# Lower steps for the last weights' pieces, the first tile's softmax first, half of the last stores on the scalar engine

## The chip, the cores and the metric

One NeuronCore of one Trainium2 chip runs the whole program. The metric is the device time of one execution in microseconds (us). Engines in the profile: PE is the tensor engine's matmuls, PEld its weight loads, DVE the vector engine, ACT the scalar engine, POOL the GpSimd engine, SP the sync engine, which issues all the DMAs of the kernel before (SPq in the rows).

## The reference

Two attention blocks with 32 learned queries, then two MLPs on 12480 tokens of 128 features with 2048 hidden features:

```
h  = softmax(I x^T / sqrt(128)) x          # I: 32 x 128, x: 12480 x 128
a  = softmax(x h^T / sqrt(128)) h          # 12480 x 128
y1 = (relu(a w_in) + alpha * min(a w_in, 0)) w_out
y2 = relu(y1 w2_in)^2 w2_out
```

The four weights come as float64 and are converted on the chip from their two 32-bit halves; x, the queries and alpha are float32.

## The kernel before

**Tiling.** The second attention and the two MLPs run over 30 tiles of 416 tokens; the hidden features are cut in 16 chunks of 128. The main loop has a step for each pair of a tile and a chunk (480, plus some at the end). At step s, `l1_a(s)` computes a chunk of the first MLP's hidden features (L575), `l2_a` a chunk of the second MLP's (L593 to L595, 24 steps later), and `l1_b` and `l2_b` add earlier chunks into the outputs y1 and y2 (L604 for the first tile, else L593 to L595). Products at full precision take three matmuls of float32r halves (hi and lo): ACT writes hi, DVE or POOL writes lo.

**Banks.** `l1_a` of the first 24 steps writes one of four PSUM banks in turn, so step s waits until ACT and DVE have read the bank of step s - 4. `l2_a(0)` at step 24 needs y1 of the first tile as `y1h` (ACT, L616) and `y1l` (DVE, L618), which follow `end_y1(0)` at step 22.

**Order.** Tile's scheduler is off (`manual_schedule`): each engine works through its instructions in program order. What does not belong to the loop's body is dealt to steps by `at(step, f)`, and runs at the end of that step's list.

**The weights' pieces.** Each weight is converted in pieces of 512 columns. `load_w` issues a DMA of 512 KB into one of four `raw` buffers (SP; L154 for w_out and w2_out, L158 for w_in and w2_in), and waits there until POOL is through with that buffer's last piece. `to_f32` has four stages: magnitude (ACT, L172, needs the DMA), low (ACT, L175), bits (DVE, L179), sign (DVE L183, then POOL L184). A fifth stage splits the result in hi and lo (ACT L218 or L204, or DVE L218; then POOL L189). For w_out there is one more POOL instruction between (L199, `aw`). `convs[4]` to `convs[7]` are the four pieces of w_out. The eight pieces of w2_in and w2_out are dealt by the table `PIECES`: piece n does its stages at five steps, and when four stages are done the load of piece n + 3 is issued. Pieces 0, 1, 2 and 4 are of w2_in, pieces 3, 5, 6 and 7 of w2_out.

**The second attention's tiles.** `first` is the softmax of tile 0: scores (PE, L435), a chain on DVE with one exponential on ACT (L443 to L465), a spreading matmul (L489), a split into `a_s` (L496, L498). Without `a_s` step 0 cannot start. `second` is the softmax of tiles 1 to 3 in six steps and a split: `a_hi` on ACT (L474), `a_lo` on POOL (L189), and twelve DMAs from SP (L480) that copy both into three `a_s` tiles. Tile 1 is needed at step 16.

**The product of the weights.** `step_u` (PE, L550, steps 11 to 14), `copy_u` (ACT, L557, `u_sb`, step 15) and `step_v` (PE, L561, step 16) form a small matrix that `end_y1` uses. L561 stands in PE's queue between the matmuls of step 16, and waits for `u_sb`.

**The end.** The last tile's y2 is transposed by DVE (L653) and stored by four DMAs from SP (L657).

Of the kernel before, what the change touches and what calls it, by code (L numbers as in the profile page):

```python
# [28 lines left out]
def attention_then_two_mlps(ctx: ExitStack, tc, x, inducing, w_in, w_out, alpha, w2_in, w2_out, out):  # L29
# [3 lines left out]
    nc = tc.nc  # L33
# [6 lines left out]
    NT = N // T  # L40
# [150 lines left out]
    def conv_w_in(k):  # L191
        return to_f32("w_in", k, lambda: w_in_sb[:, k * 512 : (k + 1) * 512])

    def conv_w_out(k):
        chunks, cols = slice(4 * k, 4 * k + 4), slice(k * 512, (k + 1) * 512)
        f, hi, lo, a = (v.rearrange("p c d -> p (c d)")[:, cols] for v in (w_out_sb, wo_hi, wo_lo, aw))

        def rest():
            nc.gpsimd.tensor_tensor(  # L199
                aw[:, chunks], w_out_sb[:, chunks], al1[:, chunks].unsqueeze(2).to_broadcast([P, 4, P]), op=ALU.mult  # L200
            )

        def split():
            nc.scalar.copy(hi, a)  # L204
            pool_lo(lo, a, hi)

        return to_f32("w_out", k, lambda: f) + [rest, split]
# [56 lines left out]
    last = len(groups1) - 1  # L264
# [65 lines left out]
    def run(fs):  # L330
        for v in fs:
            v()

    convs = [conv_w_in(k) for k in range(4)] + [conv_w_out(k) for k in range(4)]
# [32 lines left out]
    def transpose_w_in(k):  # L367
        b = y2_bank()
        for i in range(4):
            c = 4 * k + i  # L370
            nc.tensor.transpose(b[:, i * P : (i + 1) * P], w_in_sb[:, c * P : (c + 1) * P], ident)
        for i in range(4):
            c = 4 * k + i
            nc.scalar.activation(
                wiT[:, c * P : (c + 1) * P], b[:, i * P : (i + 1) * P], AF.Copy, scale=al[:, c : c + 1]
            )
# [37 lines left out]
        den.unsqueeze(1).to_broadcast([P, Q, M]), op=ALU.mult,  # L414
    )
    transpose_w_in(1)
    run(convs[5][2:4])
    convs[4][4]()


    a_s = {}
# [84 lines left out]
    def make_w1s(k):  # L506
        w1_bank[k] = x_banks[k]() if k < 2 else y2_bank()
        nc.tensor.matmul(w1_bank[k], hT, w_in_sb[:, k * 512 : (k + 1) * 512], start=True, stop=True)

    def split_w1s(k, low):  # L510
        dst, b = w1s[:, k * 512 : (k + 1) * 512], w1_bank[k]
        if low:
            nc.vector.tensor_tensor(dst[64:], b[64:], f32(dst[64:]), op=ALU.subtract)
        else:
            nc.scalar.copy(dst, b)

    first = second_attention([0], [0, P, 2 * P, T - P])
    second = second_attention([1, 2, 3])
    first[0]()
    make_w1s(0)  # L520
    transpose_w_in(2)
    run(convs[6][:2])
    run(first[1:4])
    split_w1s(0, 0)
    second[0]()
    transpose_w_in(3)
    stage1.close()
    make_w1s(1)
    convs[5][4]()
    run(first[4:6])  # L530
    split_w1s(0, 1)
    first[6]()
    convs[6][2]()
    first[7]()
    convs[6][3]()
    convs[6][4]()
    second[1]()
    split_w1s(1, 0)
    load_w("w2_in", 0)
    load_w("w2_in", 1)  # L540
# [51 lines left out]
    def three(b, w_hi, w_lo, hi, lo, start, stop):  # L592
        nc.tensor.matmul(b, w_hi, hi, start=start, stop=False)  # L593
        nc.tensor.matmul(b, w_lo, hi, start=False, stop=False)  # L594
        nc.tensor.matmul(b, w_hi, lo, start=False, stop=stop)  # L595
# [46 lines left out]
    def l2_b(i):  # L642
        t, c = divmod(i, NCH)
        if c == 0:
            y2_cur[t] = y2_bank()
        b = y2_cur[t][:, :T]
        hi, lo = g2.pop(i)
        cols = slice(c * P, (c + 1) * P)
        three(b, w2[2][:, cols], w2[3][:, cols], hi, lo, c == 0, c == NCH - 1)
        if c == NCH - 1:  # L650

            o = wk.tile([P, T], F32, name="o", tag="o", bufs=2)
            nc.vector.transpose(o, b)  # L653
            del y2_cur[t]
            dst = out[t * T : (t + 1) * T, :].rearrange("(b i) (a j) -> a i b j", i=M, j=M)
            for a in range(P // M):
                nc.sync.dma_start(  # L657
                    out=dst[a], in_=o[a * M : (a + 1) * M, :].rearrange("i (b j) -> i b j", j=M)
                )

# [1 line left out]
    SPLIT1, U_AT = [9, 11, 15, 18], [11, 12, 13, 14]  # L662

    PIECES = [
        (6, 15, "w2_in", 0), (9, 17, "w2_in", 1), (12, 19, "w2_in", 2), (15, 22, "w2_out", 0),
        (18, 24, "w2_in", 3), (21, 27, "w2_out", 1), (24, 30, "w2_out", 2), (28, 34, "w2_out", 3),
    ]
    total = NT * NCH
    plan = {}
# [1 line left out]
    def at(s, f, *a):  # L671
        plan.setdefault(s, []).append(lambda: f(*a))

    at(1, split_w1s, 1, 1)
    at(0, second[2])
    at(2, make_w1s, 2)
    at(2, split_w1s, 2, 0)
    at(2, second[3])
    at(2, second[4])
    at(5, split_w1s, 2, 1)  # L680
    at(4, second[5])
    at(2, convs[7][0])
    at(5, convs[7][1])
    at(5, convs[7][2])
    at(5, make_w1s, 3)
    at(5, split_w1s, 3, 0)
    at(7, split_w1s, 3, 1)
    at(7, second[6])
    at(7, convs[7][3])
    at(8, convs[7][4])  # L690
    for k in range(4):
# [23 lines left out]
    def stages(parts, steps):  # L715
        for v, s in zip(parts, steps):
            at(s, v)

    at(3, load_w, *PIECES[2][2:])


    def piece(n):
        s, last, name, k = PIECES[n]
        stages((conv_w2_in if name == "w2_in" else conv_w2_out)(k), [s, s + 1, s + 2, s + 3, last])
        if n + 3 < len(PIECES):
            at(s + 4, load_w, *PIECES[n + 3][2:])

    for n in range(len(PIECES)):
        at(PIECES[n][0] - 1, piece, n)
    l1_b_at = {}  # L730
    for i in range(total):
        early = max(0, min(LAG1_EARLY - LAG1, (LAG2 - 1 - i) // 2))
# [1 line left out]
    for s in range(total + LAG2 + LAG2B + 4):  # L734
        if s < total:
            l1_a(s, s < LAG2 and s % 2)
        if 0 <= s - LAG2 < total:
            l2_a(s - LAG2)
        if 0 <= s - LAG2 - 1 < total:
            l2_split(s - LAG2 - 1)  # L740

        ends = [(l1_b, i) for i in l1_b_at.get(s, [])]
        if 0 <= s - LAG2 - LAG2B < total:
            ends.insert(0 if ends and ends[0][1] % NCH == 0 else len(ends), (l2_b, s - LAG2 - LAG2B))
        for f, i in ends:
            f(i)
        for f in plan.pop(s, []):
            f()
# [30 lines left out]
```

## Time and profile before

| | |
|---|---|
| runs | 990.95, 991.48, 992.05 us; median 991.48 |
| the profiled execution | 992.0 us, of which the span from first to last instruction is 990.2 |
| busy share of the span | PE 98%, PEld 95%, ACT 77%, DVE 69%, POOL 56% |
| chain that ended last | PE 95%, DVE 1%, ACT 1%, DMA 1%, POOL 1% |
| granted TensorE clock, mean | 0.993 |

The 1.8 us between the span and the profiled execution's time lie around the program. A row of the trace has the start in us, the duration in us, the engine, the line, the operation, output and inputs, the count, and in brackets the idle time of the engine before it with what ended it. PE's matmuls overlap: two that follow each other at full speed start 0.19 us apart.

### The profile page before, as it was taken

The numbers are of one execution on the slowest core, as the hardware profiler recorded it, in microseconds if no ns is written. First come the engines' busy times: TensorE is split into PE (matmuls) and PEld (weight loads), VectorE is DVE, ScalarE is ACT, GpSimd is POOL, SyncE is SP. The second block draws the span as 40 slices with busy tenths as digits, with TensorE's granted clock in tenths as the row PEclk, the third lists the DMA queues.
The fourth block names the chain that finished last, engine by engine and source line by source line (L and its number), as shares of the span: only waits on it lengthen the run. The fifth ranks groups of instructions, "written<-read, shape, count | busy, mean of one in ns | idle before, by whom it ended". The sixth has DMA issues, their size and how long they took to land.

```text
span 990.2 us, 16031 instructions
## 1 busy us (share of the span) xinstructions
PE 971.3 (98%) x5325; PEld 937.3 (95%) x5325; DVE 685.1 (69%) x1199; ACT 762.0 (77%) x1584; POOL 556.4 (56%) x518
## 2 busy tenths in 40 slices
PE   7898999999999999999999999999999999999997
PEld 5667999999999999999999999999999999999997
DVE  4778876667666677666776667766677666776677
ACT  4757787777877777777777777777777777777776
POOL 1367766555655556555565555655556555565530
PEclk9988999999999999999999999999999999999999
DMA  9431002000010000100001000010000100010001
GB/s 315 159 97 58 1 9 44 10 10 2 10 42 10 10 9 5 40 10 10 10 12 33 10 10 10 18 27 10 9 9 23 23 10 10 9 27 1 10 9 19
DMA packets 66356, 28.42 MB, mean 29 GB/s; under 512 B 54224, under 2 KB 62176, under 8 KB 66272
## 3 DMA queue, kind: packets, MB, share of 16 engines
q1 hardware_dynamic: 66272, 27.39, 11.2%
q8 instruction: 42, 0.69, 0.3%
q14 instruction: 42, 0.34, 0.1%
HBM read 14.80 MB, written 6.39 MB: 21 GB/s over the span
## 4 chain that ended last, share of the span: by engine, by line
PE 95%; DVE 1%; ACT 1%; DMA 1%; POOL 1%; issue 0%; SPq 0%; ACTq 0%; POOLq 0%; DVEq 0%
PE y L595 18%; PE y L594 18%; PE y L593 18%; PE h L595 9%; PE h L593 9%; PE h L594 9%; PE h L575 9%; PE h L243 1%; PE ms L255 1%; PE ms L435 1%; DMA xg<-in_x_dram 1%; PE y L614 1%; PE y L316 1%; DMA raw<-in_moe_w_out_dram 0%; PE y L307 0%
## 5 line engine op out<-in xcount | busy, mean ns | idle before, releaser
L639 POOL TENSOR_TENSOR g2l<-sq,g2h 128x416 fp32r<-128x416 f32 x456 | 495.6, 1088 | 346.3 <-ACT g2h L637 235.7
L589 DVE SCALAR_TENSOR_TENSOR g1l<-h,g1h 128x416 fp32r<-128x416 f32 x464 | 274.0, 590 | 223.0 <-ACT g1h L587 218.5
L587 ACT ACTIVATE g1h<-h 128x416 fp32r<-128x416 f32 x464 | 240.4, 519 | 138.7 <-PE h L575 131.5
L631 DVE TENSOR_TENSOR sq<-h,r 128x416 f32<-128x416 f32 x480 | 283.6, 591 | 48.1 <-ACT r L629 3.0
L629 ACT ACTIVATE r<-h 128x416 f32<-128x416 f32 x480 | 249.1, 519 | 53.3 <-PE h L595 6.6
L637 ACT CAST g2h<-sq 128x416 fp32r<-128x416 f32 x480 | 255.0, 531 | 1.9 <-DVE sq L631 1.9
L575 PE MATMUL h<-a_s,w1s 128*128 128x416 f32 (+1 forms) x480 | 173.5, 363 | 2.3 <-DVE a_s L498 1.2
L595 PE MATMUL h<-y1l,w2i_hi 128*128 128x416 f32 x480 | 168.4, 351 | 1.3 <-DVE y1l L618 1.3
L593 PE MATMUL h<-y1h,w2i_hi 128*128 128x416 f32 x480 | 168.3, 351 | 1.0 <-DVE g1l L589 1.0
L595 PE MATMUL y<-g2l,w2o_hi 128*128 128x416 f32 x480 | 168.7, 351 | 0.0
L594 PE MATMUL h<-y1h,w2i_lo 128*128 128x416 f32 x480 | 168.6, 351 | 0.0
L594 PE MATMUL y<-g2h,w2o_lo 128*128 128x416 f32 x480 | 168.0, 350 | 0.0
L593 PE MATMUL y<-g2h,w2o_hi 128*128 128x416 f32 x480 | 167.7, 349 | 0.0
L595 PE MATMUL y<-g1l,wo_hi 128*128 128x416 f32 x464 | 163.1, 351 | 0.0
L594 PE MATMUL y<-g1h,wo_lo 128*128 128x416 f32 x464 | 162.7, 351 | 0.0
L593 PE MATMUL y<-g1h,wo_hi 128*128 128x416 f32 x464 | 162.4, 350 | 0.0
L575 PEld LDWEIGHTS h<-a_s,w1s 128*128 128x128 f32 (+1 forms) x480 | 90.8, 190 | 13.5 <-DVE sq L631 4.8
L593 PEld LDWEIGHTS h<-y1h,w2i_hi 128*128 128x128 f32 x480 | 90.2, 188 | 3.2 <-ACT y1h L616 1.2
L595 PEld LDWEIGHTS h<-y1l,w2i_hi 128*128 128x128 f32 x480 | 90.4, 188 | 2.0 <-DVE y1l L618 1.8
L595 PEld LDWEIGHTS y<-g2l,w2o_hi 128*128 128x128 f32 x480 | 90.1, 188 | 0.6 <-DVE g2l L639 0.3
L593 PEld LDWEIGHTS y<-g2h,w2o_hi 128*128 128x128 f32 x480 | 90.1, 188 | 0.6 <-ACT g2h L637 0.2
L594 PEld LDWEIGHTS y<-g2h,w2o_lo 128*128 128x128 f32 x480 | 90.1, 188 | 0.5
(124 smaller groups left out, 775.0 us busy)
## 6 DMA issues: line engine op xcount, KB each, us to landing
out_dram<-o SPq DMA_DIRECT2D x120, 52.0 KB, 1.9
xg<-in_x_dram SPq DMA_DIRECT2D x10, 512.0 KB, 7.2
raw<-in_moe_w_in_dram SPq DMA_DIRECT2D x8, 512.0 KB, 6.5
raw<-in_moe_w_out_dram SPq DMA_DIRECT2D x8, 512.0 KB, 3.9
a_s<-a_hi SPq DMA_DIRECT2D x58, 52.0 KB, 1.9
a_s<-a_lo SPq DMA_DIRECT2D x58, 52.0 KB, 1.9
xg<-in_x_dram SPq DMA_DIRECT2D x4, 256.0 KB, 3.8
xg<-in_x_dram SPq DMA_DIRECT2D x1, 96.0 KB, 4.7
```

The costliest lines, as they stand in the source:

```text
L243: nc.tensor.transpose(b[:, k * p : (k + 1) * p], x_t[g][:p, i, k, :], ident[:p, :p])
L255: nc.tensor.matmul(b[i * M : (i + 1) * M, :n], indT, xT[:, t0 : t0 + n], start=True, stop=True, tile_position=(0, i * M),)
L575: nc.tensor.matmul(b[:, :T], w1s[: a.shape[0], c * P : (c + 1) * P], a, start=True, stop=True)
L587: nc.scalar.activation(hi, b[:, :T], AF.Relu)
L589: nc.vector.scalar_tensor_tensor(lo, b[:, :T], 0.0, f32(hi), op0=ALU.max, op1=ALU.subtract)
L593: nc.tensor.matmul(b, w_hi, hi, start=start, stop=False)
L594: nc.tensor.matmul(b, w_lo, hi, start=False, stop=False)
L595: nc.tensor.matmul(b, w_hi, lo, start=False, stop=stop)
L629: nc.scalar.activation(r, b, AF.Relu)
L631: nc.vector.tensor_tensor(sq, b, r, op=ALU.mult)
L637: nc.scalar.copy(hi, sq)
L639: (nc.vector if i >= total - LAG2 else nc.gpsimd).tensor_tensor(lo, sq, f32(hi), op=ALU.subtract)
```

## The change

Three things. In the prologue, the instructions of tile 0's softmax go ahead of the conversion of w_out on each engine: two stages of `convs[5]`, one of `convs[4]` and those of `convs[6]`, a transposition of w_in and `make_w1s(1)` come later than before. The softmax of tiles 1 to 3 (`second`) starts later, at steps 2, 3, 4, 5, 7 and 9. The table `PIECES` gives each piece five steps of its own, lower than before; the loads come with the fourth of them. Of the last tile's four stores, two are issued by ACT. (Line numbers of the kernel after are 1 or 2 off those of before: L480 is L479, L557 is L559, L582 is L584, L587 is L589.)

```diff
     transpose_w_in(1)
-    run(convs[5][2:4])
-    convs[4][4]()
+    convs[5][2]()
...
     make_w1s(0)
-    transpose_w_in(2)
-    run(convs[6][:2])
     run(first[1:4])
     split_w1s(0, 0)
+    transpose_w_in(2)
     second[0]()
+
+    run(first[4:6])
+    first[6]()
+    convs[5][3]()
+    split_w1s(0, 1)
+    run(convs[6][:1])
+    first[7]()
+    convs[4][4]()
+    convs[6][1]()
     transpose_w_in(3)
     stage1.close()
     make_w1s(1)
+    convs[6][2]()
     convs[5][4]()
-    run(first[4:6])
-    split_w1s(0, 1)
-    first[6]()
-    convs[6][2]()
-    first[7]()
     convs[6][3]()
     convs[6][4]()
-    second[1]()
     split_w1s(1, 0)
...
-                nc.sync.dma_start(
+
+                (nc.scalar if t == NT - 1 and a % 2 else nc.sync).dma_start(
...
-        (6, 15, "w2_in", 0), (9, 17, "w2_in", 1), (12, 19, "w2_in", 2), (15, 22, "w2_out", 0),
+        ((3, 4, 5, 7, 13), "w2_in", 0), ((5, 6, 8, 9, 15), "w2_in", 1), ((8, 9, 11, 14, 16), "w2_in", 2),
+        ((11, 12, 13, 16, 21), "w2_out", 0), ((13, 14, 15, 17, 18), "w2_in", 3), ((16, 17, 18, 19, 23), "w2_out", 1),
...
-    at(7, second[6])
+    at(9, second[6])
...
-    at(3, load_w, *PIECES[2][2:])
+    at(0, load_w, *PIECES[2][1:])
...
-        s, last, name, k = PIECES[n]
-        stages((conv_w2_in if name == "w2_in" else conv_w2_out)(k), [s, s + 1, s + 2, s + 3, last])
+        steps, name, k = PIECES[n]
+        stages((conv_w2_in if name == "w2_in" else conv_w2_out)(k), steps)
         if n + 3 < len(PIECES):
-            at(s + 4, load_w, *PIECES[n + 3][2:])
+            at(steps[3], load_w, *PIECES[n + 3][1:])
```

POOL from the last aw of the prologue on, before (`a` with `sm` is the softmax of tiles 1 to 3, `a_lo` its split; `w_out_sb` and `wf` are converted pieces, w_out's last and w2's):

```order
L199 TENSOR_TENSOR aw<-w_out_sb,al_117 128x512
L461 TENSOR_TENSOR a_720<-a_720,sm 96x416
L189 TENSOR_TENSOR a_lo<-a2t,a_hi 96x416
L184 TENSOR_TENSOR w_out_sb<-mag,raw 128x512
L199 TENSOR_TENSOR aw<-w_out_sb,al_117 128x512
```

and after:

```order
L199 TENSOR_TENSOR aw<-w_out_sb,al_117 128x512
L460 TENSOR_TENSOR a_744<-a_744,sm 96x416
L184 TENSOR_TENSOR w_out_sb<-mag,raw 128x512
L184 TENSOR_TENSOR wf<-mag,raw 128x512
L199 TENSOR_TENSOR aw<-w_out_sb,al_117 128x512
L189 TENSOR_TENSOR a_lo<-a2t,a_hi 96x416
```

Three instructions of the conversion stand ahead of `a_lo` that stood behind it.

SP at the end of the twelve DMAs of tiles 1 to 3, before (the last two of the twelve, then the loads of w2_out 0, which is piece 3, of w2_in 3, which is piece 4, and of pieces 5 to 7):

```order
L480 DMA a_s<-a_hi 32x416
L480 DMA a_s<-a_lo 32x416
L154 DMA raw<-in_moe_w_out_dram 128x4x256
L158 DMA raw<-in_moe_w_in_dram 128x1024
L154 DMA raw<-in_moe_w_out_dram 128x4x256 x3
```

After, the start of the twelve (the three loads ahead are pieces 0 to 2, then piece 3):

```order
L158 DMA raw<-in_moe_w_in_dram 128x1024 x3
L154 DMA raw<-in_moe_w_out_dram 128x4x256
L479 DMA a_s<-a_hi 32x416
L479 DMA a_s<-a_lo 32x416
```

and their end:

```order
L479 DMA a_s<-a_hi 32x416
L479 DMA a_s<-a_lo 32x416
L158 DMA raw<-in_moe_w_in_dram 128x1024
L154 DMA raw<-in_moe_w_out_dram 128x4x256 x3
```

Piece 3's load moved ahead of the twelve; piece 4's still stands behind them.

ACT from step 14 to step 16, before (`g_885` is step 14's, `g1h<-h_910` step 16's; the L172 is piece 3's):

```order
L582 ACTIVATE g_885<-h_883 128x416
L204 CAST wo_hi<-aw 128x512
L557 COPY u_sb<-y_849 128x128
L218 CAST w2i_hi<-wf 128x512
L172 ACTIVATE mag<-raw 128x512
L587 ACTIVATE g1h<-h_910 128x416
```

and after, from step 13 (`g_896` is step 14's, `g1h<-h_920` step 16's; the L172 is piece 4's):

```order
L218 CAST w2i_hi<-wf 128x512
L172 ACTIVATE mag<-raw 128x512
L584 ACTIVATE g_896<-h_894 128x416
L175 ACTIVATE raw<-raw 128x512
L204 CAST wo_hi<-aw 128x512
L559 COPY u_sb<-y_858 128x128
L218 CAST w2i_hi<-wf 128x512
L589 ACTIVATE g1h<-h_920 128x416
```

The magnitude of a piece of w2 stood behind `u_sb`; now that of piece 4 stands ahead of it.

## Rows read from the trace of the kernel before

**Rows 1.** The page's 40 slices of the span: PE busy tenths, granted clock.
```profile
PE   7898999999999999999999999999999999999997
...
PEclk9988999999999999999999999999999999999999
```

**Rows 2.** Busy us by engine (PE, PEld, DVE, ACT, POOL), PEclk, DMA, by stretch.
```profile
71.67:83.50 11.83, 8.63 (x32) 4.91 (x30) 8.20 (x14) 8.83 (x19) 9.86 (x8) 0.92 0.59 198
83.50:98.00 14.50, 14.46 (x62) 13.42 (x63) 13.21 (x20) 11.06 (x25) 11.35 (x10) 0.83 0.01 4
```

**Rows 3.** Timeline of PE around steps 16 to 24.
```profile
71.67 0.38 PE L561 MATMUL ms<-u_sb,hT 128*128 128x128 f32 x2
...
83.50 0.29 PEld L595 LDWEIGHTS h<-y1l,w2i_hi 128*128 128x128 f32 x1 [1.82 <-DVE y1l L618]
```

**Rows 4.** Timeline of ACT and DVE over the same steps.
```profile
70.09 0.27 ACT L557 COPY u_sb<-y 128x128 f32<-128x128 f32 x1 [0.57 <-PE y L550]
...
73.18 0.68 ACT L172 ACTIVATE mag<-raw 128x512 f32<-128x512 f32 x1 [2.31 <-DMA raw<-in_moe_w_out_dram]
...
82.87 0.57 DVE L618 TENSOR_TENSOR y1l<-y,y1h 128x416 fp32r<-128x416 f32 x1
```

**Rows 5.** Timeline of POOL and SP's queue from `a_lo` to the loads.
```profile
60.59 1.07 POOL L189 TENSOR_TENSOR a_lo<-a2t,a_hi 96x416 fp32r<-96x416 f32 x1 [3.25 <-ACT a_hi L474]
62.29 1.41 POOL L184 TENSOR_TENSOR w_out_sb<-mag,raw 128x512 int32<-128x512 int32 x1 [0.63 <-DVE mag L183]
63.78 1.37 POOL L199 TENSOR_TENSOR aw<-w_out_sb,al 128x512 f32<-128x512 f32 x1
...
61.69 0.51 SPq L480 DMA_DIRECT2D a_s<-a_lo  x1
...
69.17 0.53 SPq L154 DMA_DIRECT2D raw<-in_moe_w_out_dram  x1
```

**Rows 6.** Timeline of the first tile's softmax, with PE's row of one slice.
```profile
44.06 0.79 DVE L449 TENSOR_TENSOR a<-a,mx 128x128 f32<-128x128 f32 x1
...
46.07 1.02 PE L508 MATMUL h<-w_in_sb,hT 128*128 128x512 f32 x2
...
46.97 0.33 ACT L452 ACTIVATE a<-a 128x128 f32<-128x128 f32 x1
...
48.39 0.31 DVE L465 STREAM_TRANSPOSE a2t<-a 128x128 f32<-128x128 f32 x1
...
51.04 1.41 PE L575 MATMUL h<-a_s,w1s 96*128 96x416 f32 x3 [1.21 <-DVE a_s L498]
...
51.00:52.00 1.00, 0.96 (x3) 0.50 0.00 0
```

**Rows 7.** Groups of DVE (count, busy us, mean ns) from 46 to 62 us; timeline; its busy us.
```profile
L183 DVE SCALAR_TENSOR_TENSOR mag<-raw,mag 128x512 int32<-128x512 int32 x2 | 1.9, 950 | 0.1
...
L179 DVE TENSOR_SCALAR mag<-mag 128x512 int32<-128x512 int32 x2 | 0.9, 427 | 0.1
...
61.00 1.21 DVE L183 SCALAR_TENSOR_TENSOR mag<-raw,mag 128x512 int32<-128x512 int32 x1
...
48.70:62.21 13.51, 11.66 (x22) 0.75 0.14 43
```

**Rows 8.** Timeline of ACT: three in a row without idle time.
```profile
59.41 0.68 ACT L172 ACTIVATE mag<-raw 128x512 f32<-128x512 f32 x1
59.98 0.53 ACT L474 CAST a_hi<-a2t 96x416 fp32r<-96x416 f32 x1
60.41 0.68 ACT L175 ACTIVATE raw<-raw 128x512 int32<-128x512 uint32 x1
```

**Rows 9.** The last stores, and all stores' issue times (ns, min/median/max) and landings.
```profile
985.90 1.90 SPq L657 DMA_DIRECT2D out_dram<-o  x4
...
L657 SPq DMA_DIRECT2D out_dram<-o x120: 315/481/1592, 124.5 to 987.3; - x120
...
DMA to landing us min/median/max: 1.7/1.9/3.2
```

More of the change, by code (lines that the diff above doesn't have):

```diff
@@ L664, in attention_then_two_mlps @@
     PIECES = [
-        (6, 15, "w2_in", 0), (9, 17, "w2_in", 1), (12, 19, "w2_in", 2), (15, 22, "w2_out", 0),
-        (18, 24, "w2_in", 3), (21, 27, "w2_out", 1), (24, 30, "w2_out", 2), (28, 34, "w2_out", 3),
[3 rows of a table added]
     ]
@@ L674, in attention_then_two_mlps @@
     at(1, split_w1s, 1, 1)
-    at(0, second[2])
+    at(2, second[1])
+    at(3, second[2])
     at(2, make_w1s, 2)
     at(2, split_w1s, 2, 0)
-    at(2, second[3])
-    at(2, second[4])
+    at(4, second[3])
+    at(5, second[4])
     at(5, split_w1s, 2, 1)
-    at(4, second[5])
+    at(7, second[5])
     at(2, convs[7][0])
@@ L717, in stages @@
             at(s, v)
-    at(3, load_w, *PIECES[2][2:])
+    at(0, load_w, *PIECES[2][1:])
     def piece(n):
-        s, last, name, k = PIECES[n]
-        stages((conv_w2_in if name == "w2_in" else conv_w2_out)(k), [s, s + 1, s + 2, s + 3, last])
+        steps, name, k = PIECES[n]
+        stages((conv_w2_in if name == "w2_in" else conv_w2_out)(k), steps)
         if n + 3 < len(PIECES):
-            at(s + 4, load_w, *PIECES[n + 3][2:])
+            at(steps[3], load_w, *PIECES[n + 3][1:])
     for n in range(len(PIECES)):
-        at(PIECES[n][0] - 1, piece, n)
+        at(PIECES[n][0][0] - 1, piece, n)
     l1_b_at = {}
```

1 row of the table PIECES is left out of this document.

## The prediction

> **What bounds the kernel now.** The page's slices come first: PE is busy nine tenths or more from the fifth slice to the last but one, at full clock [rows 1]. There nothing can be won but by fewer matmuls, and the change has the same matmuls. So only two places count: the way into the loop, up to about 98 us, and the end after the last matmul. What PE has done by 98 us, not how busy it is, decides.
>
> The table of stretches shows where the way in loses. From 71.67 to 83.50, PE is busy for 8.63 of 11.83 us, and from 83.50 to 98.00 it is busy throughout, but at a mean clock of 0.83 [rows 2]; 0.17 x 14.5 = 2.5 us are lost there to the clock, which sank to its lower level after the half idle stretch ahead. The timeline says what PE waited for: the longest wait, 1.82 us of the weight load at 83.50, was for `y1l`, the first thing that the second MLP needs [rows 3]. Followed back, it leads to ACT: after `u_sb` at 70.09 it stood 2.31 us for a DMA, until 73.18, in front of the magnitude of piece 3; with that all of ACT's later work was late, and DVE's with it: `y1l` began at 82.87 and ended at 83.44 [rows 4]. The DMA was late because SP's queue works in order: it had first to issue the twelve copies of tiles 1 to 3, the first that waits for `a_lo` at 61.69; the load followed eleven copies later at 69.17 [rows 5]. From the end of `a_lo` on POOL (60.59 + 1.07 = 61.66) to ACT's release that is 73.18 - 61.66 = 11.5 us. These two rows carry the forecast.
>
> **The first tile's softmax.** DVE has the scores without their maximum at 44.06, and could go on after one exponential; ACT did other things and began it at 46.97 [rows 6]. After the change the exponential is ACT's next instruction. DVE's subtraction, which took 0.79 there beside POOL, and for which I put 0.3, as DVE's transposition of the same size took 0.31 at 48.39, ends at 44.36; the exponential then starts at 44.4, the chain is 2.55 us earlier, and `a2t` is done at 48.70 - 2.55 = 46.15. The matmuls that stood in PE's queue ahead of the spreading (a transposition and `make_w1s(1)`, of which the latter alone took 1.02 [rows 6]) now stand behind it, so that not all of the 2.55 us reach step 0; I put 2.0, between the whole and 2.55 - 1.02, so 49.0 for 51.04. PE at half clock from 51 us on [rows 6] may go too, since it idles less ahead of it. All this is worth 2 to 5 us by step 10, if nothing later waits for something else.
>
> **The pieces at lower steps.** Something later does. The order shows piece 4's load still behind the twelve copies on SP, and its magnitude on ACT at step 13, ahead of `u_sb`; before, a waiting magnitude stood behind `u_sb`. So if the load is late, ACT stands with step 14's relu, a split of w_out, `u_sb` and all relus from step 16 on queued behind, DVE and POOL starve after it, and PE stands at L561 in step 16, which wants `u_sb`. How late is it? The copies begin in earnest with `a_lo`. On POOL it now follows the adds of w_out's last piece and of piece 0 and one `aw`. The first of these needs DVE's sign of w_out's last piece. That sign ended at 61.00 + 1.21 = 62.21 before [rows 7], 13.5 us after `a2t`. After the change DVE has between the same two points the same instructions and two more, a sign (mean 0.95) and a bits (0.43) [rows 7]. It was busy for 11.66 of the 13.51 us; if the two fill its idle time the sign ends 11.66 + 1.38 = 13.0 us after 46.15, if they add to it 14.9 us after: at 59.2 to 61.0. POOL's three take twice 1.41 and 1.37, and `a_lo` 1.07 [rows 5], together 5.3: it ends at 64.5 to 66.3, I take the middle, 65.3 or so, for 61.66 before. With the 11.5 us from there to ACT's release, ACT gets piece 4's magnitude at 76.8 (76.0 to 77.8).
>
> From this point ACT still has the magnitude, a relu, a low, a split and `u_sb`. ACT's own instructions overlap: an L172 of 0.68 is followed 0.57 later, a cast of 0.53 0.43 later [rows 8]. With 0.57 for the magnitude and the low, 0.43 for the relu and the split and 0.27 for `u_sb` that makes 2.3 us. L561 goes at 79.1, for 71.67 before [rows 3]: PE is 7.4 us behind, and what the earlier softmax won has gone into the wait.
>
> **From the release to y1l.** Before, ACT's release at 73.18 was followed by `y1l`'s end at 83.44, 10.3 us later. After, four more of ACT's instructions and `u_sb` come ahead of step 16's relu, 2.1 us by the same spacings; that is 12.4. DVE has a sign and a copy more ahead of `y1l`. Beside a busy POOL a sign took 1.21 at 61.00, and the copy can hardly take more than a sign [rows 7], so these add 0 (hidden in DVE's waits) to 2.4 us, and I allow 3. I take 14.0, nearer to the middle since POOL, starved until the release, has nine conversions to make up and is busy all the time. `y1l` ends at 76.8 + 14.0 = 90.8 for 83.44: 7.4 us late; from the ends 76.0 + 12.4 = 88.4 and 77.8 + 15.4 = 93.2, 5.0 to 9.8 late. The clock after it: PE is again half idle ahead, so I let the 2.5 us of before stand; if PE catches up at the lower clock while it waits anyway, they are won (-2.5). The pieces 5 to 7 end four steps earlier, which a busy PE hides either way [rows 2].
>
> **The last stores.** Four issues by SP take 1.90 us [rows 9]. With two on each engine the last should start two issues earlier, 0.95 us. The copies still move the same bytes, so I take 0.6; ends: 0.95 gained, and 1.0 lost, since no row shows ACT issuing a DMA and SP's slowest issue took 1.59 for a median of 0.48 [rows 9]. Nothing else is on ACT then. The Trainium skill, DMA: Bandwidth & Descriptors, section "Issuing engines are not separate DMA queues", says that issuing from several engines saves only the sequencer's time to issue, usually little beside the transfer; here it is 1.90 beside a landing of 1.9, not little. The Trainium skill, Perfetto Trace Analysis, section "DMA Instruction — HWDGE (DVE, Sync)", has the descriptor generator locked by one sequencer at a time; by that the gain would be nothing and the sum 0.6 higher. No row here shows two engines issuing.
>
> **The sum.** +7.4 - 0.6 = +6.8 against the profiled execution's 992.0 (span 990.2, 1.8 around it): 998.8. That execution was 0.5 above the median of 991.48, so the forecast is 991.48 + 6.8 = 998.3. From the ends: 5.0 - 2.5 - 0.95 = +1.6 (993.0) to 9.8 + 1.0 = +10.8 (1002.3).
>
> **The rivals.** *As meant: no late DMA reaches PE.* Then 2.0 us at step 0, 0 to 3.4 of half clock (I take 1.5), the 2.31 us of ACT's wait and 0.6 at the end are won, 6.4 us: 985. This is faster. It decides at one point: `y1l` is earlier than 83.44 only if ACT's release comes by 83.44 - 12.4 = 71, so `a_lo` ends by 59.5, ahead even of the sign that POOL waits for. Only if DVE runs through its queue 5 us faster than before, or SP issues the twelve in half the time, does that hold. Against it stands the time from 61.69 to 69.17 for eleven copies, 0.68 each [rows 5]. I give 0.08.
> *The wait is there, but is paid back.* ACT and POOL have more conversions behind them at step 24, PE works off its queue at the lower clock while it waits, and the 2.5 us do not come again: 990 to 993, say 991.5. For it: PE is busy for 8.63 us in the 11.83 of the stretch [rows 2], and ACT's release may find it with little left to do. Against it: the POOL work that the wait defers. 0.16, a third of it faster by over 0.2%.
> *Worse: POOL's backlog.* POOL stands from step 13 until the release, then does all splits in a row, and delays `g2l` of the second MLP as well: another 3 to 5 us, 1003. 0.06.
> *That the change doesn't do what it says* is part of the forecast: the pieces stand at lower steps, but are not done earlier.
>
> **How the numbers follow.** The forecast has 0.70 and gives 998.3; its lower end touches no change, of which I count 0.02. A measurement of this kernel tells about 0.2% (2 us) from no change. Faster by more than that: 0.08 + 0.05 = 0.13; within it: 0.11 + 0.02 = 0.13; slower: 0.74. The range reaches from 991.0, which leaves out the first rival and half of the second, to 1002.5, which leaves out the worst.
>
> **What would show it.** Right: in the profile after, ACT waits some 8 us or more for a raw DMA in front of L172 near 68 us; PE idles at L561 until about 79; `a_lo` runs at 64 to 65 behind three POOL conversions; `y1l` ends near 91; step 0 starts near 49. Wrong: `a_lo` before 60, or piece 4's load landing before PE reaches step 16. If `y1l` comes within 11 us of ACT's release, the middle term is too large.

## The result, and the profile after

The changed kernel takes 1001.56 us (median of 4 runs, 999.41 to 1002.90), the kernel before on the same chip 991.75. The ratio is 1.0098, with a 95% interval of 1.0079 to 1.0117: 9.7 us slower.

The slices of the page after, against [rows 1]: PE falls to six tenths in the third slice (nine before) and to seven in the fourth (eight before), where the clock is a step lower, and is as full as before from the fifth on.

```profile
PE   8867999999999999999999999999999999999998
...
PEclk9987999999999999999999999999999999999999
```

The table of stretches (busy us of PE, PEld, DVE, ACT, POOL, then the clock, DMA share, GB/s) puts the hole at 70 to 80 us, where PE works 2.78 us of 10 at the lower clock; before, the worst stretch of this kind was 8.63 of 11.83 [rows 2].

```profile
70.00:80.00 10.00, 2.78 (x7) 2.04 (x8) 2.38 (x5) 5.12 (x12) 3.98 (x4) 0.51 0.55 173
80.00:90.00 10.00, 7.18 (x25) 4.51 (x23) 7.71 (x13) 6.62 (x14) 8.89 (x7) 0.84 0.17 53
90.00:98.00 8.00, 7.46 (x31) 7.22 (x31) 6.89 (x11) 3.98 (x10) 4.28 (x4) 0.74 0.00 0
```

The timeline of the kernel after names what was waited for, in order of time: the start of the way in (`hT`, the h of the first attention, transposed), POOL's row up to `a_lo`, the first and the last of the copies that wait for `a_lo` with piece 4's load behind them, then ACT, PE, ACT and DVE.

```profile
39.47 0.29 DVE L412 TENSOR_TENSOR hT<-y,den 128x128 f32<-128x128 f32 x1
...
45.99 0.83 PE L577 MATMUL h<-a_s,w1s 96*128 96x416 f32 x3
...
58.12 1.61 POOL L184 TENSOR_TENSOR w_out_sb<-mag,raw 128x512 int32<-128x512 int32 x1 [3.34 <-issue]
59.69 1.48 POOL L184 TENSOR_TENSOR wf<-mag,raw 128x512 int32<-128x512 int32 x1
...
61.13 1.49 POOL L199 TENSOR_TENSOR aw<-w_out_sb,al 128x512 f32<-128x512 f32 x1
62.58 1.25 POOL L189 TENSOR_TENSOR a_lo<-a2t,a_hi 96x416 fp32r<-96x416 f32 x1
...
63.85 0.52 SPq L479 DMA_DIRECT2D a_s<-a_lo  x1
...
70.11 0.59 SPq L479 DMA_DIRECT2D a_s<-a_lo  x1
70.80 0.53 SPq L158 DMA_DIRECT2D raw<-in_moe_w_in_dram  x1
...
74.89 0.66 ACT L172 ACTIVATE mag<-raw 128x512 f32<-128x512 f32 x1 [9.12 <-DMA raw<-in_moe_w_in_dram]
...
77.22 0.80 PE L563 MATMUL ms<-u_sb,hT 128*128 128x128 f32 x2 [9.03 <-ACT u_sb L559]
...
84.46 0.62 ACT L218 CAST w2i_hi<-wf 128x512 fp32r<-128x512 f32 x1 [3.16 <-POOL wf L184]
...
89.91 0.57 DVE L620 TENSOR_TENSOR y1l<-y,y1h 128x416 fp32r<-128x416 f32 x1
```

This is the forecast chain: three conversions ahead of `a_lo`, twelve copies, piece 4's load, ACT's wait of 9.12 us for the raw bytes (2.31 before, [rows 4]), PE's wait of 9.03 us for `u_sb` (none in [rows 3]), `y1l` ended at 90.48 for 83.44. ACT's wait of 3.16 us for POOL at 84.46 is new.

Absolute times must not be compared here. In the profiled execution of the kernel before, `hT`, which no part of the change touches, came 2.45 us later:

```profile
41.92 0.29 DVE L412 TENSOR_TENSOR hT<-y,den 128x128 f32<-128x128 f32 x1
```

Over all 14 kernels it starts between 39.19 and 42.38, with the same instructions ahead of it, and in each 24.6 to 24.9 us after the issue of the same two loads of x: the shift is there by their issue, and no edit made it. So the distances from `hT` are compared:

| from hT's start, us | before | forecast | after |
|---|---|---|---|
| step 0 | 9.12 | 7.1 | 6.52 |
| `a_lo` ends | 19.74 | 23.4 | 24.36 |
| ACT has the raw bytes | 31.26 | 34.9 | 35.42 |
| `y1l` ends | 41.52 | 48.9 | 51.01 |

From there little differs. The time of the profiled execution less the end of `y1l` is 992.0 - 83.44 = 908.6 us before and 999.41 - 90.48 = 908.9 after, and 907.7 to 909.5 in all the kernels below. Within these 1.8 us the end of `y1l` decides the time.

### The profile page after: what moved, and what is told of

Its sections match the earlier page's. It is cut to its first block, busy times and chain, and to the rows that moved or that the text cites. A ratio compares the mean times of both kernels' runs of the same rounds, so it can differ in the third digit from the quotient of the medians.

```text
span 997.6 us, 16030 instructions
## 1 busy us (share of the span) xinstructions
PE 970.2 (97%) x5325; PEld 937.1 (94%) x5325; DVE 687.3 (69%) x1199; ACT 763.2 (77%) x1584; POOL 555.9 (56%) x518
## 4 chain that ended last, share of the span: by engine, by line
PE 94%; DVE 2%; issue 1%; ACT 1%; DMA 1%; SPq 1%; POOL 0%; ACTq 0%; DVEq 0%; POOLq 0%
PE y L596 18%; PE y L597 18%; PE y L595 18%; PE h L597 9%; PE h L595 9%; PE h L596 9%; PE h L577 9%; PE h L243 1%; PE ms L255 1%; SPq L479 1%; PE ms L434 1%; PE y L616 1%; PE y L316 1%; DMA raw<-in_moe_w_in_dram 0%; DMA xg<-in_x_dram 0%
## 5 line engine op out<-in xcount | busy, mean ns | idle before, releaser
L589 ACT ACTIVATE g1h<-h 128x416 fp32r<-128x416 f32 x464 | 240.6, 519 | 138.8 <-PE h L577 131.7
L633 DVE TENSOR_TENSOR sq<-h,r 128x416 f32<-128x416 f32 x480 | 283.7, 591 | 51.2 <-ACT r L631 4.6
L577 PE MATMUL h<-a_s,w1s 128*128 128x416 f32 (+1 forms) x480 | 174.1, 364 | 5.4 <-DVE g1l L591 2.7
L577 PEld LDWEIGHTS h<-a_s,w1s 128*128 128x128 f32 (+1 forms) x480 | 90.8, 190 | 16.6 <-DVE sq L633 4.7
L596 PEld LDWEIGHTS h<-y1h,w2i_lo 128*128 128x128 f32 x480 | 90.4, 188 | 0.4
```

Source lines behind the costliest of these rows:

```text
L577: nc.tensor.matmul(b[:, :T], w1s[: a.shape[0], c * P : (c + 1) * P], a, start=True, stop=True)
L589: nc.scalar.activation(hi, b[:, :T], AF.Relu)
L633: nc.vector.tensor_tensor(sq, b, r, op=ALU.mult)
```

## The experiments

Each is the changed kernel with the edit shown, unless it says otherwise. "The fifth of the sixteen pieces" in an expectation is piece 4 of the table, and the third and fourth are pieces 2 and 3. "y1l" is the distance from `hT`'s start to the end of `y1l` in the profiled execution.

| kernel | ratio to before (interval) | y1l, us |
|---|---|---|
| before | 1 | 41.5 |
| after | 1.0098 (1.0079 to 1.0117) | 51.0 |
| e1_load_ahead | 1.0052 (1.0035 to 1.0070) | 45.4 |
| e2_u_sb_first | 1.0082 (1.0063 to 1.0102) | 49.2 |
| e3_a_lo_first | 1.0072 (1.0050 to 1.0094) | 49.5 |
| e4_sp_stores | 1.0098 (1.0079 to 1.0116) | 51.2 |
| e5_softmax_only | 0.9997 (0.9986 to 1.0008) | 41.7 |
| e6_pieces_only | 1.0120 (1.0106 to 1.0134) | 53.0 |
| e7_copies_late | 1.0044 (1.0030 to 1.0058) | 45.2 |
| e8_six_raw | 1.0046 (1.0031 to 1.0060) | 45.1 |
| e9_softmax_six_raw | 0.9972 (0.9962 to 0.9983) | 39.6 |
| e10_six_raw_mag | 1.0032 (1.0018 to 1.0046) | 45.1 |
| e11_six_raw_split | 1.0036 (1.0024 to 1.0047) | 44.7 |
| e12_three_early | 0.9974 (0.9963 to 0.9985) | 39.9 |

The two columns agree within 1.4 us throughout (a hundredth is 9.9 us).

**Is it the load behind the copies?** The first moves piece 4's load alone.

```diff
-            at(steps[3], load_w, *PIECES[n + 3][1:])
+            at(8 if n == 1 else steps[3], load_w, *PIECES[n + 3][1:])
```

> The kernel after, with the load of piece 4 issued at step 8, so ahead of the twelve copies on SP instead of behind them; nothing else. Theory (late load): ACT's wait of 9.1 us in front of piece 4's magnitude goes, PE passes L563 with less than 1 us of idle time, and a shorter wait of some 5 us stays in front of piece 5's magnitude, whose load still stands behind the copies; y1l comes some 7 us earlier and the time is about 994.5 (992 to 996.5). Rival (too much work): ACT, DVE and POOL have too many conversions in steps 3 to 16, and would be late with or without the load; then at most 2 us are won and the time is 999 or more.

It won about half of the loss (5.6 us at `y1l`). The timeline shows the wait gone over to the next load behind the copies, issued at 73.08:

```profile
73.08 6.22 SPq L154 DMA_DIRECT2D raw<-in_moe_w_out_dram  x3
...
77.07 0.66 ACT L172 ACTIVATE mag<-raw 128x512 f32<-128x512 f32 x1 [3.07 <-DMA raw<-in_moe_w_out_dram]
```

The second leaves the load late and puts piece 4's magnitude behind `u_sb`:

```diff
-((13, 14, 15, 17, 18), "w2_in", 3)
+((15, 16, 16, 17, 18), "w2_in", 3)
```

> The kernel after, with piece 4's steps (15, 16, 16, 17, 18) for (13, 14, 15, 17, 18): its magnitude stands behind u_sb on ACT, the load stays behind the copies. Late load: ACT waits for the same DMA until about 35.4 us after hT, but PE passes L563 without waiting, and behind the release ACT has five instructions less ahead of step 16's relu; y1l 2 to 3 us earlier, time about 999 (998 to 1000). If the block of PE at L563 were itself the price, the 9 us of it would go and the time would fall below 995. Rival (too much work): no change, 1001.5.

PE no longer waits at L563, and 1.8 us are won at `y1l`. PE waits 5.33 us at L577 instead, for a bank whose `g1l` comes behind ACT's relus of step 16 on, before which ACT now stands. So that `u_sb` was hit is the small part; ACT still stands for 7.54 us.

```profile
76.52 0.66 ACT L172 ACTIVATE mag<-raw 128x512 f32<-128x512 f32 x1 [7.54 <-DMA raw<-in_moe_w_in_dram]
...
78.26 0.72 PE L577 MATMUL h<-a_s,w1s 128*128 128x416 f32 x1 [5.33 <-DVE g1l L591]
```

The third gives the second softmax its old steps, so that `a_lo` is again first on POOL:

```diff
+    second[1]()
...
-    at(2, second[1])
-    at(3, second[2])
+    at(0, second[2])
...
-    at(9, second[6])
+    at(7, second[6])
```

> The kernel after, with the softmax of tiles 1 to 3 at the steps of before (0, 2, 2, 4, 7), so that a_lo stands ahead of the three POOL conversions and the copies start earlier; the loads of pieces 3 and 4 both behind the copies. Late load: a_lo ends some 5 us earlier, and ACT's last release with it (a_lo's end + 11.5 for the first load behind the copies, 0.6 more for the second): time about 997 (995 to 999). Rival (too much work): the softmax competes with the conversions as before, 1000 to 1002.

`a_lo` ends at 61.55, 19.5 us after `hT` as in the kernel before, and ACT is released 11.7 us after it, by a load behind the copies (now piece 3's). Yet only 1.5 us are won at `y1l`: ACT then waits 3.85 us for POOL at the split.

```profile
73.26 0.66 ACT L172 ACTIVATE mag<-raw 128x512 f32<-128x512 f32 x1 [6.71 <-DMA raw<-in_moe_w_out_dram]
...
85.56 0.62 ACT L218 CAST w2i_hi<-wf 128x512 fp32r<-128x512 f32 x1 [3.85 <-POOL wf L184]
```

**Stores and softmax apart.** The fourth has all stores on SP (`nc.sync.dma_start` for every tile).

> The kernel after, with the last tile's four stores all issued by SP as before. The split of the stores won 0.3 us by the two profiles (4.02 us from the first issue to the end of the span for 4.30): time about 1001.9. If issuing from ACT costs something outside the span, or the spread of the runs of after (999.4 to 1002.9) comes from it, this is faster, 1000 or less, and its runs lie closer together. If the stores gained nothing: no change.

The ratio is that of the changed kernel, but each of the two has an interval of 1.9 us either way, in which a gain of 0.3 or 0.6 us would not show. The profiles do show 0.3: from the first issue to the end of the span it is 4.29 us here and 4.02 in the changed kernel (below).

The fifth is the kernel before with the new order of the prologue only (the diff's part from `transpose_w_in(1)` to `split_w1s(1, 0)`, with `second[1]()` left where it was).

> The kernel before with the new order of the first tile's softmax alone; the pieces' steps, the second tile's softmax and the stores are those of before. Theory (the new order of the softmax is a gain by itself, and the loss comes from the pieces' steps): step 0 of the routing stands about 6.5 us behind the start of hT where before it stood 9.1 behind, the copies to SBUF and a_lo end some 2 us earlier, and so does ScalarE's release by the third piece's DMA (about 29 us behind hT for 31.3): 988 to 990 us, a ratio of 0.997 to 0.999. Rival (the stages of the weights that the softmax passes become late on their own account): a ratio of 1.000 to 1.003.

Neither shows: the ratio is 1 within 0.14%, and `y1l` ends 0.2 us later, not earlier. Step 0 was 6.5 us behind `hT`, 2.6 earlier, but `a_lo` ended at 58.95, 19.5 behind `hT` for 19.7. The timeline shows why: `a_lo` waits for `a_hi`, and ACT does that only after a cast of `w1s` that waits for PE. ACT's release by piece 3's load came 31.5 us behind `hT`, for 31.3 before.

```profile
55.79 0.59 ACT L514 CAST w1s<-y 128x512 fp32r<-128x512 f32 x1 [2.36 <-PE y L507]
...
57.23 0.56 ACT L473 CAST a_hi<-a2t 96x416 fp32r<-96x416 f32 x1
...
57.87 1.08 POOL L189 TENSOR_TENSOR a_lo<-a2t,a_hi 96x416 fp32r<-96x416 f32 x1 [4.26 <-ACT a_hi L473]
...
70.96 0.68 ACT L172 ACTIVATE mag<-raw 128x512 f32<-128x512 f32 x1 [2.34 <-DMA raw<-in_moe_w_out_dram]
```

The sixth is the other half: the order of the prologue and the stores of before, the pieces and the second softmax of after.

> The changed kernel without the new order of the first softmax and without ScalarE's stores: the pieces' lower steps and the second tile's softmax alone. Theory (a_lo's end carries the loss, and the softmax that goes first gives part of it back): y1l ends about 53 us behind hT, for 51.0 in the changed kernel, a ratio of 1.010 to 1.013 (1000 to 1003 beside a kernel before at 990). Rival (the early softmax loads POOL and VectorE just where w_out's last stages stand and is itself a part of the loss): a ratio of 1.004 to 1.008.

`y1l` at 53.0 and 1.0120, as the theory had it. In the changed kernel, where `a_lo` follows POOL's conversions, the early softmax does help, by 1.9 us at the end of `a_lo` (24.4 behind `hT` for 26.2 here) and 1.9 at `y1l`.

**Is the load all of it?** The seventh loads piece 4 early as the first does, and puts off the copies of tiles 2 and 3:

```diff
+                if t in (2, 3):
+                    at(18, copies, i, t)
...
+            at(8 if n == 1 else steps[3], load_w, *PIECES[n + 3][1:])
```

> The changed kernel, but the load of the fifth of the sixteen pieces stands ahead of the copies to SBUF of a_lo and its neighbours, and the copies of tiles 2 and 3 are put off to step 18, so that SyncE has half as many in one stretch. Theory (a load that stands behind copies which wait for a_lo is the whole loss): ScalarE waits at most 1.5 us for the raw bytes of any piece between 60 and 80 us, y1l ends about 42 to 43 us behind hT, a ratio of 0.998 to 1.003. Rival (ScalarE's and POOL's own backlog of the early pieces carries half of the loss): y1l at 45 to 47, a ratio of 1.004 to 1.006, as with that one load moved ahead alone.

The eighth has six raw buffers:

```diff
-        raw = cv.tile([P, 512, 2], I32, name="raw", tag="raw", bufs=4)
+        raw = cv.tile([P, 512, 2], I32, name="raw", tag="raw", bufs=6)
...
-    at(0, load_w, *PIECES[2][1:])
+    for q in (2, 3, 4):
+        at(0, load_w, *PIECES[q][1:])
...
-            at(steps[3], load_w, *PIECES[n + 3][1:])
+            at((7, 8, 14)[n], load_w, *PIECES[n + 5][1:])
```

> The changed kernel with six buffers for raw pieces in place of four: three more pieces are loaded at step 0, and no load stands behind the copies to SBUF with a stage of ScalarE waiting for it. Theory (the queue of loads behind a_lo's copies is the loss): no wait of ScalarE over 0.5 us for raw bytes between 55 and 90 us; what is left are its waits for POOL (about 3 us in all): y1l ends 41 to 44 us behind hT, 988 to 993 us beside 990, a ratio of 0.998 to 1.003. Rival (more early pieces only move the wait to POOL's conversions): a wait of over 5 us for POOL in ScalarE's row, a ratio of 1.005 or more.

In both, ACT waits for no raw bytes any more (no wait of 1 us or longer for a DMA from 55 us to `y1l`), and both stop at 45 us. The theory that the load is the whole loss falls: it carries 5.9 us of `y1l`. What is left shows in ACT's longest wait, for POOL, which is busy for 18.98 of the 20 us from 60 to 80. How busy POOL is says little by itself: in the same stretch counted from `hT` (61.5 to 81.5) it is busy for 18.45 before.

```profile
60.00:80.00 20.00, 14.77 (x70) 9.81 (x69) 16.88 (x17) 12.13 (x25) 18.98 (x15) 1.00 0.41 111
```

In the kernel before:

```profile
61.50:81.50 20.00, 18.06 (x84) 12.46 (x83) 14.40 (x22) 14.33 (x31) 18.45 (x14) 1.00 0.43 138
```

ACT's wait in the eighth:

```profile
79.50 0.62 ACT L218 CAST w2i_hi<-wf 128x512 fp32r<-128x512 f32 x1 [4.37 <-POOL wf L184]
```

**What holds the rest.** Three kernels start from the eighth. The tenth has more buffers for the magnitudes (`tag="mag", bufs=3` to `bufs=5`), for which ACT waits 3.49 and 1.42 us there.

> The changed kernel with six buffers for raw pieces (as in the run before of that kind, 45.1 us from hT to y1l) and five instead of three for the magnitudes, so that ScalarE's magnitude of an early piece does not wait until POOL has added an earlier piece (waits of 3.49 and 1.42 us there). Theory (what is left of the loss is ScalarE's wait of 4.4 us for POOL's sum of the piece whose split stands one step behind its sign): no change, y1l 44.5 to 45.5 behind hT, a ratio of 1.004 to 1.005. Rival (the missing buffers of the magnitudes hold ScalarE and carry what is left): y1l 41.5 to 43, a ratio of 0.999 to 1.002.

Those waits went, and `y1l` stayed at 45.1: it is not the buffers. The eleventh puts piece 4's split at step 20 (`(13, 14, 15, 17, 20)`, with `tag="wf", bufs=3`).

> The changed kernel with six buffers for raw pieces and the split of the fifth of the sixteen pieces at step 20 instead of 18, three steps behind its sign as in the kernel before and not one; the later split needs a third buffer for the floats of a piece, else the plan would wait for itself. Theory (ScalarE's wait for POOL's sum at that split is what is left of the loss): no wait of ScalarE over 1.5 us for POOL between 70 and 85 us, y1l ends 41 to 42.5 us behind hT, a ratio of 0.999 to 1.002. Rival (POOL is full from 58 to 82 us, and the wait only moves to the next stage of it): y1l 44 to 45.5, a ratio of 1.003 to 1.005.

The rival was right. ACT's wait for POOL's sum moved to the instruction that is now next, a magnitude:

```profile
78.05 0.67 ACT L172 ACTIVATE mag<-raw 128x512 f32<-128x512 f32 x1 [2.76 <-POOL wf L184]
```

The twelfth gives five of the eight pieces their old steps:

```diff
-        ((11, 12, 13, 16, 21), "w2_out", 0), ((13, 14, 15, 17, 18), "w2_in", 3), ((16, 17, 18, 19, 23), "w2_out", 1),
-        ((19, 20, 21, 22, 26), "w2_out", 2), ((22, 23, 24, 25, 30), "w2_out", 3),
+        ((15, 16, 17, 18, 22), "w2_out", 0), ((18, 19, 20, 21, 24), "w2_in", 3), ((21, 22, 23, 24, 27), "w2_out", 1),
+        ((24, 25, 26, 27, 30), "w2_out", 2), ((28, 29, 30, 31, 34), "w2_out", 3),
```

> The changed kernel with six buffers for raw pieces, and only the first three of the eight pieces of the last weights at the new steps; the other five have the steps of before, so that some four of POOL's sums and differences of 1.3 to 1.5 us, and ScalarE's and VectorE's stages with them, stand behind y1l again and not ahead of it. Theory (what is left of the loss without the queue of loads is POOL's backlog of the pieces dealt with early, 7 of its operations on them ahead of y1l before and 11 in the changed kernel with six buffers): y1l ends 40 to 42.5 us behind hT for 45.1 with all pieces early, a ratio of 0.997 to 1.001. Rival (the second tile's softmax at its later steps, a_lo behind w_out's last operations above all, carries what is left): y1l 44 to 45.5, a ratio of 1.003 to 1.005.

`y1l` ends 39.9 us behind `hT`, even under the theory's 40, and the kernel is faster than the eighth, and than the kernel before:

```profile
42.38 0.29 DVE L412 TENSOR_TENSOR hT<-y,den 128x128 f32<-128x128 f32 x1
...
81.68 0.57 DVE L620 TENSOR_TENSOR y1l<-y,y1h 128x416 fp32r<-128x416 f32 x1
```

Its `a_lo` ends as late as the changed kernel's (24.4 behind `hT`), and the second softmax stands at its late steps: with no load behind the copies that costs next to nothing (the ninth, below, has `a_lo` 6.0 us earlier and `y1l` only 0.3). What went are the five pieces dealt early, each with stages on ACT, DVE and POOL. That POOL is the engine of the three is argued, not shown: from ACT's waits in the eighth and the eleventh, and from a count. Ahead of `y1l`, POOL begins 11 of its operations on the pieces of w2 (L184 into `wf`, L189 into `w2i_lo` or `w2o_lo`) in every kernel that deals all pieces early, and 7 in the four others (before, the fifth, the ninth and this one); four at some 1.3 us each would be the 5.2 us won here. But the same pieces have stages on ACT and DVE too, and no run moved POOL's part alone.

The clock is a rival, and the traces speak against it. Between 44 and 60 us the twelfth is at full clock throughout, and the eighth is at the lower level from about 51 to 54.5. But the seventh is at full clock there too, and its `y1l` (45.2) is that of the eighth (45.1). From 60 to 80 us all three are at full clock; the eighth falls to the lower level again only at about 82, behind ACT's wait.

**The kernel before has the same queue.** The ninth is the fifth (before with the new prologue) with six raw buffers, pieces 2 to 4 loaded at step 0.

> The kernel before with the new order of the first softmax and six buffers for raw pieces, so that the third, fourth and fifth of the sixteen pieces are loaded at step 0 and no load stands behind the copies to SBUF with ScalarE waiting for it; the pieces' stages keep the steps of before. Theory (in the kernel before, too, the load behind the copies was what ScalarE waited for last, 2.31 us, and the early softmax gave nothing because a_lo's end and that load did not move with it): the wait for raw bytes is gone, y1l ends 39 to 40.5 us behind hT for 41.5, 988 to 990 us beside 991.6, a ratio of 0.996 to 0.999. Rival (the wait is paid back by the next one, PE's for y1l or ScalarE's for POOL): y1l again 41 to 42 behind hT, a ratio of 0.999 to 1.001.

ACT's wait of 2.34 us is gone (its magnitude of piece 3 starts at 67.51, 28.3 us behind `hT`, without a wait), `y1l` ends 2.2 us earlier than in the fifth, and the kernel is 0.28% (0.17 to 0.38) faster than before. Six buffers alone, without the new prologue, were not tried, so that how much of it the early softmax holds is open.

The distances add up in this order of undoing: the changed kernel's 51.0 less 5.9 (loads, the eighth), less 5.2 (five pieces, the twelfth), less 0.3 (the rest, the ninth), plus 2.2 (the queue of the kernel before, the fifth), less 0.2 (prologue), are before's 41.5. So of the 9.5 us, 3.7 are the load queue, by which it grew, and 5.2 the early pieces. No kernel has the five pieces late and four buffers, so how the two share the loss in another order of undoing is open.

## Why the prediction was right, and where it was off

The forecast was 998.3 us with 991.0 to 1002.5, and slower. It is slower, and 1001.56 lies in the range, near its upper end. The sum was +6.8; the ratio gives +9.7. By its steps:

- **The first softmax.** The exponential follows the subtraction at once, and step 0 came 2.6 us earlier for a forecast 2.0: right. The half clock, which I had left open, went in part: the lower level held from about 49.8 to 53.2 us, for 50.9 to 57.7 before. That the gain goes into the later wait was right for the changed kernel; that the gain alone reaches nothing (the fifth) was not foreseen.
- **`a_lo`.** Three conversions stand ahead of it, as the order showed. It ends 24.4 us behind `hT` for a forecast 23.4. Half of the 1.0 us is POOL's: I took 1.41, 1.41, 1.37 and 1.07 from [rows 5], 5.3 us; the four took 1.61, 1.48, 1.49 and 1.25, and 5.7 from start to end. The other half is a start some 0.5 us later than forecast.
- **`a_lo` to ACT's release.** Forecast 11.5, measured 11.06, and 11.0 to 11.7 in the first four experiments: right. It was the best-founded term, being read off two rows.
- **From the release to `y1l`.** Forecast 14.0 (12.4 to 15.4), measured 90.48 - 74.89 = 15.6, just outside. This is the term that was too small. I had charged 2.1 us for ACT's additional instructions, which was right: step 16's relu starts 2.7 us after the release (74.89 to 77.58) for 0.6 before (73.18 to 73.75). I had allowed 0 to 3 for DVE's beside a busy POOL; ACT's own wait of 3.16 us for POOL at 84.46 was not in it. With 10.3 + 2.1 + 3.16 = 15.6 that wait alone would fill the term, though no run took it out by itself. That the allowance for DVE nearly covered it is luck. "POOL's backlog" was a rival, but with `g2l` of the second MLP as the place; it came ahead of `y1l`, at ACT's split.
- **The clock.** I let 2.5 us of lower clock recur. Most of it did: in the 14.5 us behind `y1l` the mean clock is 0.87 for 0.83 before, 1.9 us lost for 2.5. The time behind `y1l` is all the same not shorter (908.9 for 908.6).

```profile
90.50:105.00 14.50, 14.13 (x64) 13.32 (x65) 12.52 (x21) 9.27 (x20) 10.63 (x10) 0.87 0.00 1
```

- **The stores.** Forecast -0.6, measured -0.3 in the profiles; the fourth's ratio can't tell either from nothing. The two engines' issues ran side by side and took 0.9 us where SP alone took 1.90 [rows 9]:

```profile
993.58 0.83 SPq L660 DMA_DIRECT2D out_dram<-o  x2
993.58 0.92 ACTq L660 DMA_DIRECT2D out_dram<-o  x2
```

  From the first issue to the end of the span it is 997.6 - 993.58 = 4.02 us, for 990.2 - 985.90 = 4.30 before: of the 1.0 us saved in issuing 0.3 are left. The four stores, closer together, took longer to land, on SP's queue as on ACT's (medians 2.2 and 2.4 us; the last four before, all on SP, 1.9):

```profile
out_dram<-o SPq DMA_DIRECT2D x2, 52.0 KB, 2.2
out_dram<-o ACTq DMA_DIRECT2D x2, 52.0 KB, 2.4
```

  The Trainium skill, Perfetto Trace Analysis, section "DMA Instruction — HWDGE (DVE, Sync)", states that the descriptor generator is locked for exclusive use while it works for an issue. By that rule, applied to whole issues as in the prediction, the four would have taken some 1.9 us again; they took 0.9, so if there is a lock, it holds for no more than about half of an issue here.

With +9.5 for +7.4 at `y1l` and -0.3 for -0.6 at the end, 2.4 of the 2.9 us of error are named; the rest lies within the spread of the runs. The mechanism was right but not whole: the argument had one wait as the loss and everything after it as its consequence, while the eighth shows that without that wait 3.6 of the 9.5 us at `y1l` (and nearly half by the ratio) would have stayed. `y1l` at 90.48 beside the forecast 90.8 looks better than it is; with `hT` as late as in the profiled execution before, it would be 92.9.

The rivals: "as meant" would have needed `a_lo` by 59.5, which is 17.6 us behind `hT`; it ended 24.4 behind, so it fell. "Paid back" fell: nothing is won behind `y1l`.

## What to carry to other kernels

An in-order queue passes a wait on to everything behind it: before stages are dealt to earlier steps, the loads that feed them must stand ahead of whatever waits in the issuing queue, or have buffers that let them. And earlier is not better for work that nobody waits for: off-path stages that are pulled ahead of the first result that the next phase needs take their engine's time from it. Executions are compared by the distance from a common event, not by absolute times, when the start varies.

## What the hardware showed that was not expected

A single DVE instruction can stand still through several of POOL's in a row. In the changed kernel one bits stage took 4.72 us, from 64.33 to 69.05, where the others up to 100 us took 0.41 to 1.51; POOL ran four instructions back to back beside it, and the last ended at 68.77:

```profile
64.33 4.72 DVE L179 TENSOR_SCALAR mag<-mag 128x512 int32<-128x512 int32 x1 [0.93 <-ACT mag L172]
...
67.51 1.26 POOL L189 TENSOR_TENSOR w2i_lo<-wf,w2i_hi 128x512 fp32r<-128x512 f32 x1
...
75.58 0.43 DVE L179 TENSOR_SCALAR mag<-mag 128x512 int32<-128x512 int32 x1 [5.43 <-ACT mag L172]
```

In the twelfth experiment it hit a sign, 5.98 us from 66.25, until after POOL's first gap, which came at 71.69. That kernel is fast, so this block by itself is not what makes a kernel slow. Nor does every instruction meet it: the bits stage at 58.51 in the changed kernel took 1.51 us while POOL's row had no gap either.

```profile
66.25 5.98 DVE L183 SCALAR_TENSOR_TENSOR mag<-raw,mag 128x512 int32<-128x512 int32 x1
```

The Trainium skill, SBUF — State Buffer, section "Who interferes with whom", says that where an instruction of DVE and one of POOL need the ports that the two engines share, the one that issues first has them for its whole length and the other is fully blocked. These rows agree with a full block, and add that DVE's instruction can lose to several in a row; that the ports are the reason, no run here shows.
